# Operands moved to multiples of 64 bytes, and POOL's additions of token blocks spread over slots

## The chip, the cores and the metric

One core of a Trainium2 chip runs the kernel in one launch. The metric is the device time in microseconds from start to end, the median of three runs. TensorE (PE) multiplies, VectorE (DVE), ScalarE (ACT) and GpSimd (POOL) do the element-wise work, and SyncE (SP) issues the transfers. Each engine runs its instructions in the order in which they were written, and waits for others by semaphores.

## What is computed

A clustered attention, then an MLP with a rational activation, then a mixture of eight experts whose gate is balanced by eight Sinkhorn steps. All in float32, with 2 x 768 = 1536 tokens of 512 features.

```python
scores = scale * np.matmul(q, k.transpose(0, 1, 3, 2))   # 2 x 8 heads, 768 x 768, 64 deep
scores = np.where(q_assign == k_assign, scores, -1e9)    # same cluster of 16
x = softmax(scores) @ v                                  # 1536 x 512
h = x @ w_in                                             # 512 -> 2048
x = (P(h) / (Q(h) + 1e-6)) @ w_out                       # cubic by quadratic, 2048 -> 512
P = np.exp(x @ w_gate - max)                             # 1536 x 8
for _ in range(8):
    P /= P.sum(1, keepdims=True) + 1e-9
    P /= P.sum(0, keepdims=True) + 1e-9
    P *= N / E
for e in range(8):
    out += P[:, e:e + 1] * (np.maximum(x @ w1[e], 0.0) @ w2[e])   # 512 -> 1024 -> 512
```

## The kernel before

**Three terms.** Every product of two float32 matrices is made of three matmuls with operands split in a high and a low part: high by high, high by low, low by high (`mm3`, L775). A matmul has a stationary operand, 128 x 128, loaded as weights, and a moving one of up to 512 columns. A profile row names them `out<-moving,stationary`.

**Stages.** (1) Attention, to 287 us: scores `s`, transposes `pt`, the product `v`, and for each pair of heads the cluster matching (`sim` from HQK or LQK, moving, and CH or CL, stationary). (2) The first MLP, 287 to 594 us: eight units of 256 hidden features; each makes `h` from XH, XL (moving) and wh, wl (stationary), the activation in hh and hl, and `y` from hh, hl (moving) and wh, wl (stationary). (3) The first three units of the experts, written out in slots (to 696 us): here `y` has wh, wl moving and hh, hl stationary. (4) `by_seven` (L1056), 29 units: `h` by seven products `m` instead of eight, each of 384 tokens; the sums of token blocks are T2, T3, T4 and those in XH, XL, the sums of weight blocks sh, sl (POOL and ACT make them in `pieces_s`). The results go to gh, gl, which take the buffers of hh, hl, and then 12 tiles of `y` per unit with wh, wl moving and gh, gl stationary, six matmuls a tile.

**Slots.** Stages 2 and 3 are a table: `at(t, key, fn)` (L1162) puts work in slot t, and the loop at L1204 writes out the slots one after the other. A slot of stage 3 holds, in this order: the gathering of the last slot's `y` into acc on DVE (`out2`), the extra work under key "w", twelve matmuls of `h` (`stage1`) with ACT's Relu to hh and DVE's rest to hl, one step of the gate under "g", twelve matmuls of `y` (`stage2`), and the weight work ("W", "l"). t0 (L1186) is the first slot of stage 3, which has 18, t0 to t0 + 17. From t0 + 8 on the gate step is `sink_cols` (on PE the small matmul `sk`, on DVE L767 to L773) and `sink_rows` (DVE L758 to L761): nine DVE instructions, and the next slot's `sk` needs the last, L761.

**The extra work.** `factors` (L918) makes the sums of token blocks, in two halves of 384 tokens. `whole` (L926) adds the high and the low part of a block of XH and XL on POOL (L929) into a tile r; there are four per half, written in two steps a and b. The steps c and d subtract on DVE, d to f split the results (ACT `high`, DVE `low`, L945). L1198 puts a of the first half in slot t0 + 5 and the rest over the slots to t0 + 14. L1200 puts the seven steps of `pieces_s` for the first unit of `by_seven` in slots t0 + 12 to t0 + 15: a and b are four POOL additions into sf, c and d are three ACT casts (rh, sh) and POOL's rl, e is POOL's sl, f and g split that unit's second weights (`split_w`: POOL L634 and L635 on each half).

**Order on POOL.** `split_w` of a unit's second weights is written as soon as a slot comes that has it, but its first instruction waits until PE is done with the unit that had the buffer two units ago; POOL stands still for that long.

**Places in SBUF.** Pools are stacked from the left and from the right; a tile starts where the last one ends, rounded up to 32 bytes. The right stack begins with the attention's pools and, later, those of acc, gate, hh/gh, hl/gl and sg.

Of the kernel before, what the change touches and what calls it, by code (L numbers as in the profile page):

```python
# [9 lines left out]
F32 = mybir.dt.float32  # L10
# [23 lines left out]
def kernel(  # L34
# [16 lines left out]
    P = 128  # L51
# [48 lines left out]
    def right(stack, name, bufs):  # L100
        return stack.enter_context(tc.tile_pool(name=name, bufs=bufs, side="right"))

    def psum(stack, name, bufs):
        return stack.enter_context(tc.tile_pool(name=name, bufs=bufs, space=PSUM))

    stp = right(actx, "stp", 3)
    pp = right(actx, "pp", 6)
    ptp = right(actx, "ptp", 3)
    vsp = right(actx, "vsp", 3)
    sm = right(actx, "sm", 3)  # L110
    xfp = right(actx, "xfp", 2)
    ldp = right(pctx, "ldp", 2)
    one = right(pctx, "one", 1)
# [9 lines left out]
    NB = 4 * NT  # L123
# [47 lines left out]


    csq = one.tile([P, D], F32, name="csq")
    css = one.tile([P, 1], F32, name="css")
    nc.scalar.activation(csq, cen, AF.Square, accum_out=css)
    cnm = one.tile([P, 1], F32, name="cnm")
    gt(cnm, css, half[:, 0:1], op=ALU.pow)
    nc.vector.tensor_scalar(cnm, cnm, 1e-6, None, op0=ALU.add)
    crn = one.tile([P, 1], F32, name="crn")
    nc.vector.reciprocal(crn, cnm)  # L180
    cn2 = one.tile([P, 2, D], F32, name="cn2")
    for j in range(2):
# [67 lines left out]
    def prep(n):  # L250

        b, hp = pairs[n]
# [4 lines left out]
        st = {}  # L257
# [73 lines left out]
            (nc.vector.tensor_tensor if n == 0 else gt)(sv, sv, rev, op=ALU.mult)  # L331

        def classify_d():
            mk = st["mk"] = one.tile([P, NB], F32, tag="mk", name=f"mk_{n}")
            nc.vector.tensor_reduce(mk, st["sv"], axis=AX.X, op=ALU.max)

        def classify_e():
# [31 lines left out]
        def vsplit(j):  # L369
# [19 lines left out]
            (None, classify_m),  # L389
            (None, classify_c),  # L390
            (None, classify_d),
            (classify_e, onehot if n == 0 else lambda: (onehot(), hot.append(onehot_out))),
            *([(onehot_out, None)] if n == 0 else []),
# [21 lines left out]
        return ps  # L415

    def maxima(g, i, ps):
        nm = sm.tile([P, 1], F32, tag="nm", name=f"nm_{g}_{i}")
        nc.vector.tensor_reduce(nm, ps[:, :, :HS], axis=AX.XY, op=ALU.max, negate=True)  # L419
        return nm  # L420

# [93 lines left out]
    def attention():  # L515
# [23 lines left out]
        for kk in range(END + LAGT + 9):  # L539
# [25 lines left out]
            if kk < END:  # L565
                top[kk] = maxima(*divmod(kk, GT), score[kk])
# [112 lines left out]
    for kk in attention():  # L679
# [5 lines left out]
        x = kk - LASTK  # L685
# [212 lines left out]
    PER = NCH * FT  # L898
    N1 = NU1 * PER
    NCL = 3  # L900
    NO = NU1 + NCL
# [12 lines left out]
    def xraw(k, t, j):  # L914
        c = slice(t * HT + j * JT, t * HT + (j + 1) * JT)
        return XH[:, k * K2 : (k + 1) * K2, c], XL[:, k * K2 : (k + 1) * K2, c]

    def factors():  # L918

        st = {}  # L920
        vec = nc.vector.tensor_tensor

        def half(j):
            js = slice(j * JT, (j + 1) * JT)

            def whole(k, t):  # L926
                h, l = xraw(k, t, j)
                r = st[k, t] = wq.tile([P, K2, JT], F32, tag=f"rh{t}", name=f"r_{k}{t}_{j}")
                gt(r, h.bitcast(F32), l.bitcast(F32), op=ALU.add)  # L929

            def parts(n):
                if n not in xop:
                    xop[n] = (
                        xt.tile([P, K2, HT], F32R, tag=f"t{n}h" if n < 4 else "t3", name=f"T{n}h"),
                        xt.tile([P, K2, HT], F32R, tag=f"t{n}l", name=f"T{n}l"),
                    )
                h, l = xop[n]
                return h[:, :, js], l[:, :, js]

            def high(n, r):  # L940
                nc.scalar.copy(parts(n)[0], r)

            def low(n, r):
                h, l = parts(n)
                vec(l, r, h.bitcast(F32), op=ALU.subtract)  # L945

            def a():
                whole(0, 1)
                whole(0, 0)

            def b():
                whole(1, 1)
                whole(1, 0)

            def c():
                for k in range(K2):
                    r = sums[j, k] = cp.tile([P, JT], F32, tag=f"u{2 * j + k}", name=f"T1_{j}_{k}")
                    vec(r, st[0, 1][:, k], st[0, 0][:, k], op=ALU.subtract)
                vec(st[0, 1], st[1, 1], st[0, 1], op=ALU.subtract)

            def d():
                for k in range(K2):
                    vec(st[1, 1][:, k], st[1, 1][:, k], sums[j, k], op=ALU.subtract)
                vec(st[1, 0], st[1, 1], st[1, 0], op=ALU.subtract)
                high(3, st[0, 1])

            def e():
                high(2, st[1, 1])
                high(4, st[1, 0])
                low(3, st[0, 1])  # L970

            def f():
                low(2, st[1, 1])
                low(4, st[1, 0])

            return [a, b, c, d, e, f]

        return half(0) + half(1)

    def first_factor():  # L980
# [6 lines left out]
    def pieces_s(ui):  # L987

        st = {}

        def a():
            st["w"] = staged.pop((ui, 0))
            st["s"] = cp.tile([P, 4, K2, P], F32, tag="sf", name=f"sf_{ui}")
            w, s_ = st["w"], st["s"]
            gt(s_[:, 0], w[:, 0:K2, P:], w[:, K2:, P:], op=ALU.add)
            gt(s_[:, 1], s_[:, 0], w[:, 0:K2, :P], op=ALU.subtract)

        def b():
            w, s_ = st["w"], st["s"]
            gt(s_[:, 2], w[:, 0:K2, :P], w[:, 0:K2, P:], op=ALU.subtract)  # L1000
            gt(s_[:, 3], w[:, K2:, :P], s_[:, 1], op=ALU.subtract)

        def c():
            w = st["w"]
            rh = wq.tile([P, 3, K2, P], F32R, tag="rh0", name=f"rh_{ui}")
            rl = wq.tile([P, 3, K2, P], F32R, tag="rh1", name=f"rl_{ui}")
            sh = wp.tile([P, 4, K2, P], F32R, tag="wh0", name=f"sh_{ui}")
            sl = wp.tile([P, 4, K2, P], F32R, tag="wl0", name=f"sl_{ui}")
            wop[ui] = (rh, rl, sh, sl)
            nc.scalar.copy(rh[:, 0:2].rearrange("p a k f -> p (a k) f"), w[:, :, :P])  # L1010
            nc.scalar.copy(rh[:, 2], w[:, K2:, P:])

        def d():
            w, s_ = st["w"], st["s"]
            rh, rl, sh, sl = wop[ui]
            f2 = "p a k f -> p (a k) f"
            nc.scalar.copy(sh, s_)
            gt(rl[:, 0:2].rearrange(f2), w[:, :, :P], rh[:, 0:2].rearrange(f2).bitcast(F32), op=ALU.subtract)  # L1018
            gt(rl[:, 2], w[:, K2:, P:], rh[:, 2].bitcast(F32), op=ALU.subtract)

        def e():
            rh, rl, sh, sl = wop[ui]
            gt(sl, st["s"], sh.bitcast(F32), op=ALU.subtract)

        def f():
            st["f"] = split_w(ui, 1)
            st["f"][0]()

        def g():
            st["f"][1]()  # L1030

        return [a, b, c, d, e, f, g]
# [129 lines left out]
    def at(t, key, val):  # L1162
        plan.setdefault(t, {}).setdefault(key, []).append(val)

    for ui in range(NO):
        m = units[ui][0]
        for c in range(NCH):
            for f in range(FT):
                n = ui * PER + c * FT + f
                t = n + m * SHIFT  # L1170
# [6 lines left out]
        t = ui * PER + m * SHIFT  # L1177
# [8 lines left out]
    t0 = N1 + SHIFT  # L1186
# [8 lines left out]
        if it < 7:  # L1195
            at(t0 + 8 + it, "g", lambda it=it: sink_rows(it + 1))
    assert 16 < PER * NCL
    for x, fn in enumerate(factors()):  # L1198
        at(t0 + 5 + x * 10 // 12, "w", fn)
    for x, fn in enumerate(pieces_s(NO)):  # L1200
        at(t0 + PER * (NCL - 1) + x // 2, "w", fn)

    last = t0 + PER * NCL
    for t in range(last):  # L1204
# [10 lines left out]
        if steps:  # L1215
            a, b, c, d = steps
# [65 lines left out]
```

## Time and profile before

| | us |
|---|---|
| three runs: median (lowest to highest) | 1623.37 (1623.31 to 1623.74) |
| the profiled execution | 1621.8 |
| its span, first to last instruction | 1620.0 |
| attention | 0 to 287 |
| first MLP | 287 to 594 |
| three units in slots, with the gate | 594 to 696 |
| `by_seven` | 696 to 1604 |
| last `y` tiles and output | 1604 to 1620 |

Over the span PE is busy for 1557.0 us (96%), DVE for 1211.5 (75%), POOL for 816.3 (50%), ACT for 681.6 (42%). Matmuls overlap: a `y` of 512 columns is listed with 394 ns, but the next one starts far sooner, so PE's pace is read from starts, not from durations. DMA engines are busy for a small share after the attention.

### The profile page before, as it was taken

To read this page: it belongs to the slowest core of one execution; us is meant where nothing else is said; L and a number is where in the kernel's file an instruction comes from. 1 tells how busy PE (TensorE), PEld (TensorE's weight loads), DVE (VectorE), ACT (ScalarE), POOL (GpSimd) and SP (SyncE) were. 2 spreads that over 40 slices of the span, in tenths; PEclk is the share of its full clock that TensorE was granted. 3 is DMA by queue.
4 is the path that set the end of the run, shared out by engine and by line. 5 is a ranking of instruction groups with operands and counts; after the bars stand their busy time and mean duration, and the time that the engine had idled before them with its cause. 6 is when DMAs were issued, how large, how long until landed. Compare 5 with 4: busy or idle time off the path is not lost.

```text
span 1620.0 us, 21142 instructions
## 1 busy us (share of the span) xinstructions
PE 1557.0 (96%) x7780; PEld 1353.5 (84%) x7780; DVE 1211.5 (75%) x1963; ACT 681.6 (42%) x1292; POOL 816.3 (50%) x725
## 2 busy tenths in 40 slices
PE   5999998799999999999999999999999999999999
PEld 5888887577777787788888888888888888888887
DVE  6888888899999957878666666666666666666665
ACT  4999888697777741122221212222121222212121
POOL 5577674698777894333533443353344335334420
PEclk8999999899999999999999999999999999999999
DMA  8556542121112010100110110011011001101102
GB/s 185 129 122 136 133 96 93 62 78 53 52 53 78 14 40 14 39 27 27 40 40 27 37 43 27 27 40 40 27 40 39 27 27 40 40 27 40 39 1 78
DMA packets 70950, 87.96 MB, mean 54 GB/s; under 512 B 29792, under 2 KB 48320, under 8 KB 70848
## 3 DMA queue, kind: packets, MB, share of 16 engines
q1 hardware_dynamic: 70848, 86.63, 19.1%
q8 instruction: 61, 1.00, 0.3%
q14 instruction: 41, 0.34, 0.1%
HBM read 62.97 MB, written 3.19 MB: 41 GB/s over the span
## 4 chain that ended last, share of the span: by engine, by line
PE 77%; DVE 15%; issue 4%; ACT 3%; POOL 0%; DMA 0%; SPq 0%; ACTq 0%; DVEq 0%; POOLq 0%
PE y L776 12%; PE y L778 12%; PE y L777 12%; PE m L778 9%; PE m L776 9%; PE m L777 9%; PE pt L438 2%; DVE acc L879 2%; PE v L460 2%; PE h L776 2%; PE h L777 1%; PE v L461 1%; PE h L778 1%; PE s L413 1%; DVE ptl L448 1%
## 5 line engine op out<-in xcount | busy, mean ns | idle before, releaser
L893 DVE SCALAR_TENSOR_TENSOR acc<-y,gate,acc 128x512 f32<-128x512 f32 x348 | 260.8, 750 | 198.9 <-PE y L778 198.0
L1018 POOL TENSOR_TENSOR rl<-sg,rh 128x512 fp32r<-128x512 f32 x29 | 46.1, 1590 | 540.2 <-ACT rh L1010 523.6
L776 PE MATMUL y<-wh,gh 128*128 128x512 f32 x696 | 275.5, 396 | 0.0
L777 PE MATMUL y<-wl,gh 128*128 128x512 f32 x696 | 274.5, 394 | 0.0
L778 PE MATMUL y<-wh,gl 128*128 128x512 f32 x696 | 274.5, 394 | 0.0
L1079 ACT ACTIVATE gh<-u 128x384 fp32r<-128x384 f32 x58 | 30.5, 525 | 430.2 <-DVE u L1104 430.2
L778 PEld LDWEIGHTS y<-wh,gl 128*128 128x128 f32 x696 | 130.6, 188 | 32.3
L777 PEld LDWEIGHTS y<-wl,gh 128*128 128x128 f32 x696 | 130.4, 187 | 27.0
L776 PEld LDWEIGHTS y<-wh,gh 128*128 128x128 f32 x696 | 130.5, 187 | 26.2
L776 PE MATMUL h<-XH,wh 128*128 128x512 f32 x264 | 106.4, 403 | 22.7 <-DVE hl L847 21.6
L1095 ACT COPY c<-m 128x384 f32<-128x384 f32 x58 | 27.8, 480 | 225.6 <-PE m L778 225.6
L448 DVE TENSOR_TENSOR ptl<-pt,pth 128x384 fp32r<-128x384 f32 x192 | 97.3, 548 | 29.6 <-ACT pth L447 29.5
L1079 ACT ACTIVATE gh<-v 128x384 fp32r<-128x384 f32 x174 | 91.2, 524 | 60.1 <-DVE v L1118 27.6
L1080 DVE SCALAR_TENSOR_TENSOR gl<-v,gh 128x384 fp32r<-128x384 f32 x174 | 115.7, 665 | 0.0
L778 PE MATMUL h<-XH,wl 128*128 128x512 f32 x264 | 103.8, 393 | 1.1 <-POOL wl L666 1.1
L777 PE MATMUL h<-XL,wh 128*128 128x512 f32 x264 | 103.9, 393 | 0.0
L635 POOL TENSOR_TENSOR wl<-sg,wh 128x512 fp32r<-128x512 f32 x70 | 99.0, 1414 | 5.9
L419 DVE TENSOR_REDUCE nm<-s 128x1 f32<-128x768 f32 x96 | 91.0, 948 | 6.7 <-PE s L414 5.9
L438 PE MATMUL pt<-ident,pr 128*128 128x128 f32 x576 | 85.4, 280 | 8.5 <-DVE ptl L448 8.2
L447 ACT CAST pth<-pt 128x384 fp32r<-128x384 f32 x192 | 82.7, 482 | 24.3 <-PE pt L438 23.2
L427 ACT ACTIVATE pr<-s,nm 128x768 f32<-128x768 f32 x96 | 87.7, 913 | 2.2 <-DVE nm L419 1.6
L821 POOL TENSOR_TENSOR uu<-uu,h 128x512 f32<-128x512 f32 x48 | 67.7, 1411 | 37.6 <-ACT uu L819 37.6
(226 smaller groups left out, 4280.9 us busy)
## 6 DMA issues: line engine op xcount, KB each, us to landing
sg<-in_moe_w_dram SPq DMA_DIRECT2D x64, 512.0 KB, 3.7
stg<-in_moe_w_in_dram SPq DMA_DIRECT2D x8, 1024.0 KB, 5.4
stg<-in_moe_w_out_dram SPq DMA_DIRECT2D x8, 1024.0 KB, 4.9
st<-HQK SPq DMA_DIRECT2D x16, 384.0 KB, 4.2
st<-LQK SPq DMA_DIRECT2D x32, 192.0 KB, 4.1
st<-HQK SPq DMA_DIRECT2D x32, 192.0 KB, 4.7
qk<-in_q_dram SPq DMA_DIRECT2D x16, 192.0 KB, 3.0
qk<-in_k_dram SPq DMA_DIRECT2D x16, 192.0 KB, 3.6
```

Source lines behind the costliest of these rows:

```text
L419: nc.vector.tensor_reduce(nm, ps[:, :, :HS], axis=AX.XY, op=ALU.max, negate=True)
L427: nc.scalar.activation(pr, ps[:, :, :HS], AF.Exp, bias=nm, accum_out=rss[n][:, x : x + 1])
L438: nc.tensor.transpose(ps[:, i * P : (i + 1) * P], pv_[:, j * P : (j + 1) * P], ident)
L447: nc.scalar.copy(th[:, jj, :], ps[:, :HS])
L448: nc.vector.tensor_tensor(tl[:, jj, :], ps[:, :HS], th[:, jj, :].bitcast(F32), op=ALU.subtract)
L635: gt(wl[:, c], raw[:, c], wh[:, c].bitcast(F32), op=ALU.subtract)
L776: nc.tensor.matmul(ps, ah, bh, start=first, stop=False)
L777: nc.tensor.matmul(ps, ah, bl, start=False, stop=False)
L778: nc.tensor.matmul(ps, al, bh, start=False, stop=last)
L893: nc.vector.scalar_tensor_tensor(a, ps, p, a, op0=ALU.mult, op1=ALU.add)
L1079: nc.scalar.activation(gh[:, f], c, AF.Relu)
L1080: soon.append(lambda: nc.vector.scalar_tensor_tensor(gl[:, f], c, 0.0, gh[:, f].bitcast(F32), op0=ALU.max, op1=ALU.subtract))
```

## The change

It has three parts.

1. A tile of 8 float32 (32 bytes) is put at the start of the right stack, and some small tiles that were followed by matmul operands get a size that is a multiple of 64 bytes (css, cnm, crn, mk), with a view of the old size; nm gets four buffers instead of three, so that what lies behind it keeps its place. In bytes modulo 128 (from the built programs):

| tiles | before | after |
|---|---|---|
| XH, XL, wh, wl, sh, sl, rh, rl, T2 to T4 | 64 | 64 |
| hh, hl, gh, gl | 32 | 0 |
| st, vs, pth, ptl, pr | 96 | 64 |
| HQK, LQK | 32 | 64 |
| CH, CL | 96 | 0 |
| ident, ones | 0 | 0 |

2. The four additions of a half in `factors` become four steps of their own, and the steps get slots by a list: the first half's additions in t0 + 3, 3, 4, 4 and c to f in t0 + 5 to 8; the second half's additions in t0 + 8, 9, 10, 11 and c to f in t0 + 12 to 15.

3. The seven steps of `pieces_s` go to t0 + 13, 14, 16, 16, 17, 17, 17.

```diff
+    right(ctx, "pad", 1).tile([P, 8], F32, name="pad")
     stp = right(actx, "stp", 3)
...
-    css = one.tile([P, 1], F32, name="css")
+    css = one.tile([P, 16], F32, name="css")[:, :1]
...
-            mk = st["mk"] = one.tile([P, NB], F32, tag="mk", name=f"mk_{n}")
+            mk = st["mk"] = one.tile([P, 32], F32, tag="mk", name=f"mk_{n}")[:, :NB]
...
-        nm = sm.tile([P, 1], F32, tag="nm", name=f"nm_{g}_{i}")
+        nm = sm.tile([P, 1], F32, tag="nm", name=f"nm_{g}_{i}", bufs=4)
...
-            def a():
-                whole(0, 1)
-                whole(0, 0)
-
-            def b():
-                whole(1, 1)
-                whole(1, 0)
-
...
-            return [a, b, c, d, e, f]
+            return [lambda k=k, t=t: whole(k, t) for k in range(2) for t in (1, 0)] + [c, d, e, f]
...
-    for x, fn in enumerate(factors()):
-        at(t0 + 5 + x * 10 // 12, "w", fn)
-    for x, fn in enumerate(pieces_s(NO)):
-        at(t0 + PER * (NCL - 1) + x // 2, "w", fn)
+    for x, fn in zip((3, 3, 4, 4, 5, 6, 7, 8, 8, 9, 10, 11, 12, 13, 14, 15), factors()):
+        at(t0 + x, "w", fn)
+    for x, fn in zip((13, 14, 16, 16, 17, 17, 17), pieces_s(NO)):
+        at(t0 + x, "w", fn)
```

PE's and SP's instructions stand in the same order before and after. On the others the order moves in stage 3 only. The changed file has one line more ahead of these places (L930 is the old L929) and later seven fewer.

On POOL, around the second half's additions (r_01_1 to r_10_1), before; wh_10_0 and wh_10_1 are the first and second weights of the third unit, and each half of a split is one L634 and one L635:

```order
L634 TENSOR_SCALAR wh_10_0_6885<-sg_10_0_6706 128x512
L635 TENSOR_TENSOR wl_10_0_6886<-sg_10_0_6706,wh_10_0_6885 128x512
L634 TENSOR_SCALAR wh_10_1_7039<-sg_10_1_6841 128x512
L635 TENSOR_TENSOR wl_10_1_7040<-sg_10_1_6841,wh_10_1_7039 128x512
L929 TENSOR_TENSOR r_01_1_7045<-XH_80,XL_81 128x768
L929 TENSOR_TENSOR r_00_1_7047<-XH_80,XL_81 128x768
L929 TENSOR_TENSOR r_11_1_7049<-XH_80,XL_81 128x768
L929 TENSOR_TENSOR r_10_1_7051<-XH_80,XL_81 128x768
L634 TENSOR_SCALAR wh_10_1_7039<-sg_10_1_6841 128x512
L635 TENSOR_TENSOR wl_10_1_7040<-sg_10_1_6841,wh_10_1_7039 128x512
```

and after:

```order
L635 TENSOR_SCALAR wh_10_0_6895<-sg_10_0_6710 128x512
L636 TENSOR_TENSOR wl_10_0_6896<-sg_10_0_6710,wh_10_0_6895 128x512
L930 TENSOR_TENSOR r_01_1_6953<-XH_80,XL_81 128x768
L930 TENSOR_TENSOR r_00_1_7003<-XH_80,XL_81 128x768
L635 TENSOR_SCALAR wh_10_1_7047<-sg_10_1_6850 128x512
L636 TENSOR_TENSOR wl_10_1_7048<-sg_10_1_6850,wh_10_1_7047 128x512
L930 TENSOR_TENSOR r_11_1_7053<-XH_80,XL_81 128x768
L635 TENSOR_SCALAR wh_10_1_7047<-sg_10_1_6850 128x512
L636 TENSOR_TENSOR wl_10_1_7048<-sg_10_1_6850,wh_10_1_7047 128x512
L930 TENSOR_TENSOR r_10_1_7103<-XH_80,XL_81 128x768
```

Two additions moved ahead of the split of wh_10_1, one between its halves, one behind it.

On DVE, in slot t0 + 9, from the last `y` of slot t0 + 8 on, before:

```order
L887 COPY acc_4053<-y_8_2_3_6984 128x512
L945 TENSOR_TENSOR T2l_6941<-r_11_0_6792,T2h_6940 128x2x384
L945 TENSOR_TENSOR T4l_6944<-r_10_0_6794,T4h_6943 128x2x384
L806 SCALAR_TENSOR_TENSOR hl_9_1_6948<-h_9_1_1_6997,hh_9_1_6947 128x512
L767 TENSOR_REDUCE cs_1_7014<-sk_1_7012 128x8
L770 TENSOR_SCALAR cs_1_7014<-cs_1_7014 128x8
L771 RECIPROCAL cs_1_7014<-cs_1_7014 128x8
L772 TENSOR_SCALAR cs_1_7014<-cs_1_7014 128x8
L773 TENSOR_TENSOR gate_4054<-gate_4054,cs_1_7014 128x96
```

and after:

```order
L888 COPY acc_4057<-y_8_2_3_6992 128x512
L807 SCALAR_TENSOR_TENSOR hl_9_1_6956<-h_9_1_1_7005,hh_9_1_6955 128x512
L768 TENSOR_REDUCE cs_1_7022<-sk_1_7020 128x8
L771 TENSOR_SCALAR cs_1_7022<-cs_1_7022 128x8
L772 RECIPROCAL cs_1_7022<-cs_1_7022 128x8
L773 TENSOR_SCALAR cs_1_7022<-cs_1_7022 128x8
L774 TENSOR_TENSOR gate_4058<-gate_4058,cs_1_7022 128x96
```

T2l and T4l of the first half (step f) moved to slot t0 + 8, and the gate chain from L767 on follows hl.

On ACT, from the last cast of the second half's sums (T4h) on, before:

```order
L941 CAST T4h_6943<-r_10_1_7051 128x2x384
L1010 CAST rh_11_7210<-sg_11_0_6991 128x512
L1011 CAST rh_11_7210<-sg_11_0_6991 128x256
L1017 CAST sh_11_7212<-sf_11_7156 128x1024
L805 ACTIVATE hh_10_0_7161<-h_10_0_1_7219 128x512
L805 ACTIVATE hh_10_1_7270<-h_10_1_0_7272 128x512
L805 ACTIVATE hh_10_1_7270<-h_10_1_1_7320 128x512
```

and after:

```order
L942 CAST T4h_6904<-r_10_1_7103 128x2x384
L806 ACTIVATE hh_10_1_7258<-h_10_1_0_7260 128x512
L806 ACTIVATE hh_10_1_7258<-h_10_1_1_7308 128x512
L1003 CAST rh_11_7347<-sg_11_0_6999 128x512
L1004 CAST rh_11_7347<-sg_11_0_6999 128x256
L1010 CAST sh_11_7349<-sf_11_7206 128x1024
L806 ACTIVATE hh_10_2_7356<-h_10_2_0_7358 128x512
```

The casts of rh and sh moved behind the Relu of three more slots, T4h behind one.

## Rows read from the trace of the kernel before

**Rows 1.** Busy times by stage: span, then each engine (instructions), PEclk, DMA, GB/s

```profile
640.00:696.00 56.00, 49.04 (x211) 39.28 (x210) 46.35 (x97) 10.38 (x18) 21.95 (x21) 0.97 0.09 29
696.00:1604.00 908.00, 908.00 (x4509) 813.80 (x4508) 608.65 (x997) 192.84 (x373) 340.81 (x304) 1.00 0.10 33
```

**Rows 2.** The same view, three units of the first MLP

```profile
399.80:510.66 110.86, 103.24 (x433) 80.17 (x432) 110.65 (x145) 82.85 (x127) 86.32 (x55) 1.00 0.18 59
```

**Rows 3.** Timeline of PE: start us, us, instruction; first and last of 48 h

```profile
286.78 0.39 PE L776 MATMUL h<-XH,wh 128*128 128x512 f32 x1
...
297.43 0.39 PE L778 MATMUL h<-XH,wl 128*128 128x512 f32 x1
```

**Rows 4.** Timeline of PE: first of 18 y, and the m behind them

```profile
1006.22 0.40 PE L776 MATMUL y<-wh,gh 128*128 128x512 f32 x1
...
1010.41 0.33 PE L776 MATMUL m<-XH,rh 128*128 128x384 f32 x1
```

**Rows 5.** Timeline of PE: first and tenth y of a group, first MLP

```profile
404.22 0.40 PE L776 MATMUL y<-hh,wh 128*128 128x512 f32 x1
...
406.32 0.40 PE L776 MATMUL y<-hh,wh 128*128 128x512 f32 x1
```

**Rows 6.** Timeline of PE: four starts of sim apart, five of v

```profile
93.06 0.33 PE L297 MATMUL sim<-HQK,CL 128*128 128x384 f32 x1
...
93.75 0.34 PE L297 MATMUL sim<-LQK,CH 128*128 128x384 f32 x1
...
285.74 0.33 PE L460 MATMUL v<-pth,vs 128*128 128x384 f32 x1
...
286.60 0.34 PE L461 MATMUL v<-ptl,vs 128*128 128x384 f32 x1
```

**Rows 7.** Groups of instructions on DVE, first MLP: busy us, mean ns, idle before

```profile
L844 DVE TENSOR_TENSOR res<-uu,q 128x512 f32<-128x512 f32 x48 | 32.4, 675 | 0.3
L840 DVE TENSOR_TENSOR hh<-uu,h 128x512 fp32r<-128x512 f32 x48 | 32.4, 674 | 4.8 <-POOL uu L822 4.8
```

**Rows 8.** Waits (us, times, longest), timeline of PE, busy times of a stretch

```profile
PE sk L765 <- DVE gate L761: 7.0, 3, 4.4
...
643.78 0.39 PE L778 MATMUL h<-XH,wl 128*128 128x512 f32 x1
...
649.40:652.70 3.30, 3.30 (x9) 2.54 (x8) 3.02 (x12) 0.00 (x0) 1.80 (x3) 0.50 0.46 155
```

**Rows 9.** Timeline of DVE: T4l, the late gate chain, an undisturbed one

```profile
638.53 2.59 DVE L945 TENSOR_TENSOR T4l<-r,T4h 128x768 fp32r<-128x768 f32 x1
...
641.64 0.24 DVE L767 TENSOR_REDUCE cs<-sk 128x8 f32<-128x96 f32 x1
...
644.68 1.81 DVE L773 TENSOR_TENSOR gate<-gate,cs 128x96 f32<-128x96 f32 x1
...
647.29 1.13 DVE L761 TENSOR_TENSOR gate<-gate,rs 128x96 f32<-128x96 f32 x1
...
657.39 0.25 DVE L767 TENSOR_REDUCE cs<-sk 128x8 f32<-128x96 f32 x1
...
659.38 0.26 DVE L761 TENSOR_TENSOR gate<-gate,rs 128x96 f32<-128x96 f32 x1
```

**Rows 10.** Timeline of POOL: additions of both halves, a half split

```profile
603.53 7.24 POOL L929 TENSOR_TENSOR r<-XH,XL 128x768 f32<-128x768 f32 x4
...
635.80 0.62 POOL L634 TENSOR_SCALAR wh<-sg 128x512 fp32r<-128x512 f32 x1 [17.54 <-PE y L778]
636.50 1.29 POOL L635 TENSOR_TENSOR wl<-sg,wh 128x512 fp32r<-128x512 f32 x1
637.75 8.62 POOL L929 TENSOR_TENSOR r<-XH,XL 128x768 f32<-128x768 f32 x4
```

**Rows 11.** Groups of instructions on ACT and POOL in by_seven

```profile
L1017 ACT CAST sh<-sf 128x1024 fp32r<-128x1024 f32 x28 | 29.0, 1035 | 0.0
...
L1023 POOL TENSOR_TENSOR sl<-sf,sh 128x1024 fp32r<-128x1024 f32 x28 | 76.3, 2726 | 0.0
```

More of the change, by code (lines that the diff above doesn't have):

```diff
@@ L173 @@
     csq = one.tile([P, D], F32, name="csq")
-    css = one.tile([P, 1], F32, name="css")
+    css = one.tile([P, 16], F32, name="css")[:, :1]
     nc.scalar.activation(csq, cen, AF.Square, accum_out=css)
-    cnm = one.tile([P, 1], F32, name="cnm")
+    cnm = one.tile([P, 16], F32, name="cnm")[:, :1]
     gt(cnm, css, half[:, 0:1], op=ALU.pow)
     nc.vector.tensor_scalar(cnm, cnm, 1e-6, None, op0=ALU.add)
-    crn = one.tile([P, 1], F32, name="crn")
+    crn = one.tile([P, 16], F32, name="crn")[:, :1]
     nc.vector.reciprocal(crn, cnm)
```

## The prediction

> **What bounds the kernel now.** I read the profile stage by stage: first the busy times of each engine in the stages, then the starts of single matmuls, because the durations of pipelined matmuls overlap and only the distance from one start to the next is time that is paid. From 696 to 1604 us, the loop `by_seven`, PE is busy for 908.00 of 908.00 us and no other engine comes near [rows 1]: a nanosecond on each matmul there is a nanosecond on the end. Between 640 and 696 us PE is busy for 49.04 of 56.00 us [rows 1], so it waits for something. In the first MLP it is different again: in three of its units DVE is busy for 110.65 of 110.86 us [rows 2], and PE follows it. So there are two questions: what one matmul costs in the last 908 us, and what PE waits for ahead of them.
>
> **One matmul.** Where `h` is made, 512 columns at a time, 47 starts take 297.43 - 286.78 = 10.65 us, 226.6 ns each [rows 3]. Where `y` is made in `by_seven`, with 512 columns and three terms too, 18 starts take 1010.41 - 1006.22 = 4.19 us, 232.8 ns each [rows 4]. What differs is the place of the operands. For `h` the moving operand (XH, XL) and the stationary one (wh, wl) both lie 64 past a multiple of 128 bytes. For `y` the moving one (wh, wl) does too, but the stationary one (gh, gl) lies 32 past, so the two stand 32 bytes apart. In the first MLP's `y` the moving operand (hh, hl) is the displaced one, and there nine starts take 406.32 - 404.22 = 2.10 us, 233.3 ns each [rows 5]: the same surcharge from the other side. The displacement by itself does not cost it: in the attention both operands of `v` lie 32 past a multiple of 64, and five starts of 384 columns take 0.86 us, 172 ns each [rows 6]; 226.6 ns less 128 columns at 2.4 GHz (53.3 ns) is 173. So I read it as a surcharge on the distance between the two read streams, 232.8 - 226.6 = some 6.3 ns on 512 columns.
>
> **Part 1, the pad and the tile sizes.** After the change gh and gl lie at multiples of 128 and wh, wl still 64 past one: the distance goes from 32 to 64. The trace has no 512-column matmul at that distance; the nearest row is `sim` with 384, HQK at 32 and CH at 96 past a multiple of 128, where four starts take 93.75 - 93.06 = 0.69 us, 172 ns each [rows 6], no surcharge. So I take it as gone, 226.6 ns; the ends that I keep are no change at all and the same 6.3 ns on the other side.
> - `by_seven`: 29 units x 12 tiles x 6 = 2088 matmuls of `y` x 6.3 ns = 13.2 us, all on the path [rows 1].
> - The three plain units ahead of it: 36 tiles x 6 = 216 x 6.3 ns, 1.3 us on PE's path between its waits.
> - The first MLP: 576 x 6.7 ns would be 3.9 us, but DVE is the bound there [rows 2]. I take 0: DVE's own work covers it, and 3.9 us is the end of the range if it does not.
> - The attention: scores and `v` have distance 0 before and after; 0.
> - Other engines use the moved tiles too. On DVE, L840 writes hh (at 32) in 674 ns and L844 writes res (at 0) in 675 ns [rows 7]; a moved tile is worth nothing there, and I take the same for ACT and POOL. The wider css, cnm, crn and mk, the pad and the fourth buffer of nm change no instruction and no order: 0.
>
> The Trainium skill has a rule against this part. "TensorE: Matmul & The Clock Gate", Part 2, the first of its steps, says that PE reads the moving operand and the weights through two independent ports, so that loading the next weights takes no bandwidth from the running matmul. By it no distance between the two could matter, and part 1 would be worth 0. The rows of `h` and `y` do differ [rows 3, 4], so I keep it as a rival only.
>
> **Part 2, one addition per slot.** Ahead of `by_seven` PE waits for the gate at `sk`: 7.0 us in three waits, the longest 4.4, until L761 [rows 8], the last of a chain of nine small DVE instructions. Undisturbed the chain takes 659.38 + 0.26 - 657.39 = 2.25 us; in the late one it takes 647.29 + 1.13 - 641.64 = 6.78, L773 alone 1.81, and ahead of it T4l takes 2.59 [rows 9]. All that time POOL is in four additions of L929 in a row, 8.62 us, and L773 ends at 646.49, 0.1 us behind them (646.37) [rows 9, 10]. I read it so: a DVE instruction whose operands lie in SBUF waits until the POOL instruction that is running ends. After the wait the granted clock is 0.50, the 1.2 GHz level, for the 3.3 us of [rows 8], which costs half of that, 1.6 us; 0.97 over the stage [rows 1] is one such stretch. Together 8.6 us.
>
> After the change two of these four additions stand on POOL ahead of the split of wh_10_1, for which POOL waits until 635.80 [rows 10], and fall into idle time; the other two alternate with the split's halves; and T2l and T4l leave this slot of DVE. POOL's run from 635.80 on is two halves (0.62 + 1.29 each) and two additions (7.24 / 4 = 1.81 undisturbed [rows 10]), 7.4 us, where it was 12.4. I laid the chain over that run: it starts when hl is done, no longer behind T2l and T4l; L772 then waits for a half, L773 for the last addition, until 643.2, and the rest for what POOL does next. By this estimate it ends near 644.8, 0.8 us after PE is ready (643.78 + 0.23 [rows 8]); I take a wait of 1.0 us, and the clock as staying up. The two later waits go: the casts of rh and sh move behind three more hh on ACT, and with them rl, sl and the second weights' split move behind the last gate chain. Gain 8.6 - 1.0 = 7.6 us; the ends are 8.6 (no wait) and 2.6 (the long wait stays, with its clock).
>
> Who waits for what was moved: `by_seven` needs sl for its second product. Three casts (sh's is the longest, 1.04 us), rl and sl (sl's is the longest, 2.73 us [rows 11]) are under 8.6 us behind slot 15's hh, and PE still has two and a half slots to run, each 12 x 226.6 + 12 x 226.6 ns = 5.4 us: 13 us. That cover of 5 us gone, the loop would start late by what is missing, once. DVE's c, d, e, f stand a slot earlier (first half) or later (second), as much work in a slot as before, in slots where PE did not wait for it: 0.
>
> **Sum.** 13.2 + 1.3 + 7.6 = 22.1 us. The profiled execution took 1621.8 us (span 1620.0) and would take 1599.7; the median of the three timed runs is 1623.37, and there it is 1601.3 us. A measurement of this kernel can tell 0.2%, 3.2 us, from no change.
>
> **Rivals.**
> - Phase stays: the surcharge has another cause, `y` keeps 232.8 ns, and part 2 alone works. For it: no 512-column row at distance 64, and 384 columns may hide a surcharge that 512 show. Against it: `sim`, and the same surcharge for both kinds of `y`. 1623.4 - 7.6 = 1615.8. The Trainium skill would have it so by a second rule: "SBUF — State Buffer", Specifications (TRN2), gives lines of 16 bytes, and to these an offset of 32 is as good as one of 64.
> - Stall moves: part 1 works, but POOL is still busy for 7.4 us in a row, and if the chain meets it at every link, as before, `sk` waits its 4.4 us, the clock falls, and the later waits come back beside wh_10_1 and sf. 1623.4 - 14.5 = 1608.9.
> - Slower: the surcharge grows with the distance, and 64 costs twice what 32 does. Then 2088 + 216 `y` cost another 6.3 ns each, 14.5 us, against the 7.6 of part 2: 1623.4 + 6.9 = 1630.3. It decides from 7.6 us / 2304 = 3.3 ns more on each `y`, at 236 ns. `sim` speaks against it.
> - Neither does what it says: `y` stays and the stall moves; 1623.4, within 0.2%.
>
> **How the numbers follow.** Forecast 0.64, phase stays 0.14, stall moves 0.12, slower 0.06, neither 0.04. The forecast's own range is 1597 (no wait left, and the first MLP gives most of its 3.9 us) to 1607 (the long wait stays). The range goes on to 1616.5 and takes in the second and third case: 1597 to 1616.5. Faster by over 0.2%: 0.90; within 0.2%: 0.04; slower: 0.06.
>
> **What would show it.** Right: `y` starts 226 to 227 ns apart in `by_seven`; that loop 13 us shorter; one `sk` wait of about 1 us and no stretch at clock 0.50 between 640 and 660 us; the first MLP as long as before. Wrong: `y` at 233 ns or more; the chain to L761 still over 4 us beside POOL's additions; PE idle at the start of `by_seven`.

## The result, and the profile after

The changed kernel takes 1604.16 us (median of four runs, 1603.78 to 1604.57) beside 1623.55 for the kernel before on the same chip: a ratio of 0.988, 95% interval 0.9863 to 0.9897. The prediction was 1601.3, in a range of 1597 to 1616.5. The profiled execution has a span of 1602.3 us where it was 1620.0, 17.7 less; the medians lie 19.4 apart, because the profiled execution of before was 1.6 us under the median of its timed runs, and this difference is not traced to a place.

Busy times of the changed kernel by stretch (span, then PE, PEld, DVE, ACT, POOL with instructions, PEclk, DMA, GB/s): the end of the three units, `by_seven`, and three units of the first MLP, which answer to [rows 1, 2].

```profile
640.00:686.00 46.00, 45.02 (x203) 36.91 (x203) 38.99 (x90) 9.82 (x17) 16.38 (x17) 1.00 0.11 35
686.00:1586.00 900.00, 900.00 (x4511) 814.56 (x4511) 611.08 (x998) 193.36 (x375) 341.22 (x304) 1.00 0.10 33
398.90:510.00 111.10, 103.14 (x434) 80.09 (x433) 110.89 (x145) 83.06 (x128) 86.70 (x55) 1.00 0.17 57
```

PE now idles for 1 us in the first stretch, its clock is 1.00 there, PE is the bound in `by_seven` as before, and DVE in the first MLP as before.

Timeline of PE of the changed kernel (start us, us, instruction): the first and the tenth `y` of a group in the first MLP, the first `y` of a group in `by_seven` and the `m` behind its 18, against [rows 5] and [rows 4].

```profile
403.58 0.39 PE L777 MATMUL y<-hh,wh 128*128 128x512 f32 x1
...
405.68 0.39 PE L777 MATMUL y<-hh,wh 128*128 128x512 f32 x1
...
1001.59 0.39 PE L777 MATMUL y<-wh,gh 128*128 128x512 f32 x1
...
1005.72 0.33 PE L777 MATMUL m<-XH,sh 128*128 128x384 f32 x1
```

In the first MLP nine starts still take 2.10 us, 233.3 ns each: nothing has changed there. In `by_seven` 18 starts take 4.13 us, 229 ns each, where they took 4.19. Over all 2088 the three lines differ: y<-wh,gh starts 229 ns before its follower, y<-wl,gh 232, y<-wh,gl 226, in an exact cycle of three. So the surcharge is neither gone nor kept.

The three stages end here (same view, the last `y` of the first MLP, the first `m` and the last `y` of all), first in the changed kernel and then in the kernel before:

```profile
593.36 0.39 PE L779 MATMUL y<-hh,wl 128*128 128x512 f32 x1
...
686.98 0.33 PE L777 MATMUL m<-XH,rh 128*128 128x384 f32 x1
...
1598.25 0.39 PE L779 MATMUL y<-wh,gl 128*128 128x512 f32 x1
```

```profile
593.93 0.40 PE L778 MATMUL y<-hh,wl 128*128 128x512 f32 x1
...
696.01 0.33 PE L776 MATMUL m<-XH,rh 128*128 128x384 f32 x1
...
1615.94 0.39 PE L778 MATMUL y<-wh,gl 128*128 128x512 f32 x1
```

From the first to the second is the stage of the three units, 93.6 us where it was 102.1; from the second to the third `by_seven` with its last tiles, 911.3 us where it was 919.9. These two lengths are used for all experiments below, since they leave out the attention: the first `h` behind it starts between 286.0 and 288.3 us in the profiled executions of this document, before and after, so its length is not put down to the change.

The stall, in waits of PE (us, times, longest), PE's timeline around it, then DVE's and POOL's:

```profile
PE sk L766 <- DVE gate L762: 1.0, 1, 1.0
```

```profile
643.01 0.39 PE L779 MATMUL h<-XH,wl 128*128 128x512 f32 x1
644.37 0.43 PE L766 MATMUL sk<-gate,ones 128*128 128x96 f32 x2 [0.97 <-DVE gate L762]
```

```profile
639.73 1.10 DVE L773 TENSOR_SCALAR cs<-cs 128x8 f32<-128x8 f32 x1
640.86 1.85 DVE L774 TENSOR_TENSOR gate<-gate,cs 128x96 f32<-128x96 f32 x1
...
643.64 0.59 DVE L762 TENSOR_TENSOR gate<-gate,rs 128x96 f32<-128x96 f32 x1
```

```profile
639.51 1.29 POOL L636 TENSOR_TENSOR wl<-sg,wh 128x512 fp32r<-128x512 f32 x1
640.76 1.84 POOL L930 TENSOR_TENSOR r<-XH,XL 128x768 f32<-128x768 f32 x1
```

One wait of 1.0 us is left of the three in [rows 8]. The chain has the shape that the prediction laid out: L773 ends with the half split (640.83 and 640.80 us), L774 (1.85 us) with the last addition (1.84 us; 642.71 and 642.60), and L762 is done at 644.23.

### The profile page after: what moved, and what is told of

It reads as the page before. It is cut to its first block, busy times and chain, and to the rows that moved or that the text cites. A ratio compares the mean times of both kernels' runs of the same rounds, so it can differ in the third digit from the quotient of the medians.

```text
span 1602.3 us, 21124 instructions
## 1 busy us (share of the span) xinstructions
PE 1545.0 (96%) x7780; PEld 1351.9 (84%) x7780; DVE 1208.5 (75%) x1963; ACT 682.4 (43%) x1292; POOL 815.9 (51%) x725
## 4 chain that ended last, share of the span: by engine, by line
PE 76%; DVE 14%; issue 4%; ACT 3%; POOL 2%; DMA 0%; SPq 0%; ACTq 0%; DVEq 0%; POOLq 0%
PE y L778 12%; PE y L777 12%; PE y L779 11%; PE m L779 9%; PE m L777 9%; PE m L778 9%; PE pt L439 2%; DVE acc L880 2%; PE v L461 2%; PE v L462 1%; PE s L414 1%; PE h L777 1%; DVE ptl L449 1%; DVE q L827 1%; PE h L778 1%
## 5 line engine op out<-in xcount | busy, mean ns | idle before, releaser
L779 PE MATMUL y<-wh,gl 128*128 128x512 f32 x696 | 270.2, 388 | 0.0
```

The source lines that it names most:

```text
L779: nc.tensor.matmul(ps, al, bh, start=False, stop=last)
```

## Experiments

**The two parts apart.** `places_only` has the pad and the tile sizes with the old lists of slots; `slots_only` has the new lists with the old places:

```diff
-    for x, fn in zip((3, 3, 4, 4, 5, 6, 7, 8, 8, 9, 10, 11, 12, 13, 14, 15), factors()):
-        at(t0 + x, "w", fn)
-    for x, fn in zip((13, 14, 16, 16, 17, 17, 17), pieces_s(NO)):
-        at(t0 + x, "w", fn)
+    for x, fn in enumerate(factors()):
+        at(t0 + 5 + x * 10 // 12, "w", fn)
+    for x, fn in enumerate(pieces_s(NO)):
+        at(t0 + PER * (NCL - 1) + x // 2, "w", fn)
```

> Only the places of the operands are changed (pad and tile sizes); the slots of GpSimd's additions and of the first unit's pieces are those of the kernel before. Theory (the two parts are independent): y as in the changed kernel, 229, 232 and 226 ns for its three lines in by_seven, which makes that loop about 8.5 us and the y of the three units about 0.7 us shorter; the long wait at sk (4 to 5 us), the stretch at clock 0.50 and the later waits stay. About 1623.5 - 9.2 = 1614.3 us. Rival (most of the gain of by_seven comes from the new slots, because its weights are ready when it starts): y stays near 233 ns and the time is 1622 or more.

> Only the slots are changed; all operands lie where they lay in the kernel before. Theory: y stays at 233 ns in by_seven and in the three units; one wait at sk of about 1.1 us is left, no stretch at clock 0.50, and the three units end about 7.8 us earlier: about 1623.5 - 7.8 = 1615.7 us. Rival (the shorter y moved PE against DVE and did part of it): the wait at sk is longer than 2 us and the time is above 1618.

Waits of PE and the ends of the stages, `places_only`, then `slots_only`:

```profile
PE sk L766 <- DVE gate L762: 7.0, 3, 4.4
```

```profile
696.09 0.33 PE L777 MATMUL m<-XH,rh 128*128 128x384 f32 x1
...
1607.35 0.39 PE L779 MATMUL y<-wh,gl 128*128 128x512 f32 x1
```

```profile
PE sk L765 <- DVE gate L761: 1.0, 1, 1.0
```

```profile
688.53 0.33 PE L776 MATMUL m<-XH,rh 128*128 128x384 f32 x1
...
1608.46 0.39 PE L778 MATMUL y<-wh,gl 128*128 128x512 f32 x1
```

| kernel | median us | ratio to before (95%) | three units | `by_seven` to last `y` | waits at `sk` |
|---|---|---|---|---|---|
| before | 1623.18 | 1 | 102.1 | 919.9 | 7.0 |
| places_only | 1614.44 | 0.9945 (0.993 to 0.9959) | 101.7 | 911.3 | 7.0 |
| slots_only | 1613.55 | 0.994 (0.9925 to 0.9954) | 94.1 | 919.9 | 1.0 |
| changed | 1604.16 | 0.988 (0.9863 to 0.9897; its before: 1623.55) | 93.6 | 911.3 | 1.0 |

The parts are independent: the places are worth 8.6 us in `by_seven` and 0.4 in the units, the slots 8.0 us in the units and nothing in `by_seven`. Both rivals fall. The expectation for `slots_only`, 1615.7, was 2 us too high; by the stages it gained 8.0 instead of 7.8, and the rest lies between medians and profiled executions and is not traced.

**What distance is free.** In `shift64` and `shift192` a second pad moves hh, hl, gh and gl alone:

```diff
+    right(ctx, "pad2", 1).tile([P, 16], F32, name="pad2")    # 48 in shift192
     hb = right(ctx, "hb", 3)
```

> The changed kernel with 64 bytes more ahead of hh, hl, gh, gl: the distance from the stationary gh, gl to the moving wh, wl is then 0 modulo 128 and 128 modulo 256 (changed kernel: 64 modulo 128; before: 96 modulo 128). Theory A (what costs is the distance modulo 128, and only 0 is free): y starts 226 to 227 ns apart on all three lines in by_seven, 2088 x 2.2 = 4.6 us less there and some 0.8 us less in the three units, and the y of the first MLP at 226.6 ns without a gain in time: about 1598.8 us. Theory B (a longer period): y stays at 228 ns or more, 1603 or more. Theory C (only the stationary operand's own place counts, and 64 is enough): as the changed kernel, 229, 232 and 226 ns, 1604.2 us.

> The changed kernel with 192 bytes more ahead of hh, hl, gh, gl: the distance from gh, gl to wh, wl is then 0 modulo 512, as between XH and wh, where h is made. Theories A and B (distance): y starts 226 to 227 ns apart in by_seven and in the first MLP, about 1598.8 us; A and B differ in shift64 alone. Theory C (only the stationary operand's own place counts, and 64 is enough): as the changed kernel, 1604.2 us. If y still takes more than 228 ns on two of its lines, no distance explains it and another cause must be sought, such as the order in which the three terms follow each other.

They took 1611.92 us (ratio 0.9928, 0.9914 to 0.9943) and 1603.01 (0.9873, 0.9856 to 0.9889). So 0 modulo 128 is not enough (theory A falls), and 0 modulo 512 gave only a fifth of the gain expected (1.15 us under the changed kernel instead of 5.4). None of that fifth is in `by_seven`, which takes 911.2 us in `shift192` beside 911.3 (918.3 in `shift64`). Timeline of PE, `shift64`: first `y` of a group and the `m` behind its 18.

```profile
1005.15 0.39 PE L778 MATMUL y<-wh,gh 128*128 128x512 f32 x1
...
1009.33 0.34 PE L778 MATMUL m<-XH,sh 128*128 128x384 f32 x1
```

`shift192`: two `y` of the first MLP, nine starts apart, then the first and the tenth `y` of a group in `by_seven` and the `m` behind it:

```profile
404.13 0.39 PE L778 MATMUL y<-hh,wh 128*128 128x512 f32 x1
...
406.17 0.39 PE L778 MATMUL y<-hh,wh 128*128 128x512 f32 x1
...
1008.91 0.39 PE L778 MATMUL y<-wh,gh 128*128 128x512 f32 x1
...
1010.99 0.39 PE L778 MATMUL y<-wh,gh 128*128 128x512 f32 x1
...
1013.03 0.33 PE L778 MATMUL m<-XH,rh 128*128 128x384 f32 x1
```

At distance 0 the first nine `y` of a group take 2.08 us, 231 ns each, and the other nine 2.04 us, 226.7 each. In the first MLP, too, they take 2.04 us where they took 2.10. So distance 0 is free once the stream has settled, and in `by_seven`, where groups of 18 `y` follow `m` of 384 columns, half of each group goes by before it has. That makes the mean 228.9 ns over 18, the same as in the changed kernel, which never settles and pays in a cycle of three. `shift64` takes 4.18 us for 18, 232 ns.

Three more kernels give the three buffers of gh (and of gl) three distances in one kernel, by a larger tile for each buffer and a pool of its own for hl and gl, with pads between:

```diff
-    hb = right(ctx, "hb", 3)
+    right(ctx, "pad2", 1).tile([P, 64], F32, name="pad2")
+    hbl = right(ctx, "hbl", 3)
+    right(ctx, "pad3", 1).tile([P, 80], F32, name="pad3")
+    hb = right(ctx, "hb", 3)
+
+    def part(pool, tag, name, n):
+        return pool.tile([P, FT * 512 + 16], F32R, tag=tag, name=name)[:, : FT * n].rearrange(
+            "p (f n) -> p f n", f=FT
+        )
...
-                            hb.tile([P, FT, JT], F32R, tag="hh", name=f"gh_{ui}_{j}_{t}"),
-                            hb.tile([P, FT, JT], F32R, tag="hl", name=f"gl_{ui}_{j}_{t}"),
+                            part(hb, "hh", f"gh_{ui}_{j}_{t}", JT),
+                            part(hbl, "hl", f"gl_{ui}_{j}_{t}", JT),
```

(the second of the three; the others have 8 for 16 and pads of 16 and 104, and of 48 and 104). Each was run once, so they are read by their starts and not by their times.

> The changed kernel with the three buffers of hh (gh) and of hl (gl) each at another distance from the moving wh, wl: stationary less moving address is 32, 64 and 96 modulo 512 for units that follow each other. So far by_seven's y takes, as a mean of a group: 233 ns at 224 (before), 229 at 192 (changed kernel), 232 at 128 (shift64), and at 0 (shift192) it starts with nine slower ones and then stays at 226.7. Theory P256 (the cost repeats every 256 bytes and only 0 settles at 226.7): 229 ns or more at all three. Theory SMALL (near distances are as good as 0, since the weights are read just behind or ahead of the moving stream): 32 and 64 settle at 226.7. Theory SIZE (what counts is the largest power of two that divides the distance): 32 and 96 like 224, 233 ns; 64 like 192, 229 ns.

> As the run before, with distances of 256, 320 and 384 modulo 512. Theory P256 (the cost repeats every 256 bytes): 256 settles at 226.7 ns like 0, 384 is like 128 (232 ns, never settling), 320 is 228 ns or more. Theory P512: 256 does not settle. Theory SIZE (the largest power of two that divides the distance): 320 like 192 (229 ns), 384 like 128 (232), 256 better than both.

> As the two runs before, with distances of 416, 448 and 480 modulo 512. Theory P256 (the cost repeats every 256 bytes): 448 shows the three lines of the changed kernel, 229, 232 and 226 ns; 480 shows the 233 ns of the kernel before; 416 is 228 or more. Theory SIZE: 448 the same, 416 and 480 both 233. Theory P512: none of them has to look like an earlier one.

Timeline of PE, `map_256_320_384`: first `y` of a group and the `m` behind its 18, for 320, 256 and 384 in this order.

```profile
1003.66 0.39 PE L786 MATMUL y<-wh,gh 128*128 128x512 f32 x1
...
1007.86 0.34 PE L786 MATMUL m<-XH,sh 128*128 128x384 f32 x1
...
1012.04 0.39 PE L786 MATMUL y<-wh,gh 128*128 128x512 f32 x1
...
1016.16 0.33 PE L786 MATMUL m<-XH,rh 128*128 128x384 f32 x1
...
1019.31 0.39 PE L786 MATMUL y<-wh,gh 128*128 128x512 f32 x1
...
1023.48 0.34 PE L786 MATMUL m<-XH,sh 128*128 128x384 f32 x1
```

18 starts take 4.20, 4.12 and 4.17 us. The same rows of `map_32_64_96` at 64 and of `map_416_448_480` at 448, 4.20 and 4.12 us:

```profile
1006.39 0.39 PE L786 MATMUL y<-wh,gh 128*128 128x512 f32 x1
...
1010.59 0.34 PE L786 MATMUL m<-XH,sh 128*128 128x384 f32 x1
```

```profile
1005.12 0.39 PE L786 MATMUL y<-wh,gh 128*128 128x512 f32 x1
...
1009.24 0.33 PE L786 MATMUL m<-XH,sh 128*128 128x384 f32 x1
```

Every group of one distance agrees with the others within 0.1 ns, so a table can be made, of the stationary operand's address less the moving one's (from the built programs), modulo 256, and the mean from one start to the next over a group of 18:

| distance | 0 | 32 | 64 | 96 | 128 | 160 | 192 | 224 |
|---|---|---|---|---|---|---|---|---|
| ns | 228.9 | 233.2 | 233.3 | 234.0 | 232.0 | 233.3 | 228.9 | 233.0 |
| seen at (modulo 512) | 0, 256 | 32 | 64, 320 | 96 | 128, 384 | 416 | 192, 448 | 224 (before), 480 |

P256 holds in every pair that was run: 256 settles as 0 does, 448 has the changed kernel's cycle of three, 384 repeats `shift64`, 480 the kernel before; 32, 96 and 160 were seen at one distance each. SMALL falls (32 and 64 cost all of it), and so does SIZE: 64 and 192 have the same power of two and cost 233.3 and 228.9. These two are 64 to either side of 0, so the distance has a sign. In `by_seven` the moving operand always lies in the same place, so these groups alone could as well show the stationary operand's own place. The first MLP parts the two: there the tiles have the opposite roles, wh and wl stay where they are as the stationary operand, and the pace still follows the distance. hh at 32 modulo 128 made it 32, [rows 5], the change made it 64, which costs the same 233.3, and `shift192` made it 0, 226.7. At 192, in two of the three kernels above, the starts there come to the cycle of 229, 232 and 226 ns as well, after some four slower ones. Why these values and not others cost is not shown by any run here.

**What the slots did.** Three kernels, each run once, undo one piece of part 2 in the changed kernel: the four additions together again, the old slots for `pieces_s`, or T2l and T4l back in the slot of the late chain.

```diff
-    for x, fn in zip((3, 3, 4, 4, 5, 6, 7, 8, 8, 9, 10, 11, 12, 13, 14, 15), factors()):
+    for x, fn in zip((3, 3, 4, 4, 5, 6, 7, 8, 10, 10, 10, 10, 12, 13, 14, 15), factors()):
```

> The changed kernel with the four GpSimd additions of the second half in one slot again (t0 + 10, between the halves of a split), and everything else as changed: T2l and T4l of the first half stay out of the slot, the first unit's pieces stay late. Theory (a DVE instruction on SBUF operands waits for the running GpSimd instruction): the gate chain of that slot runs into four additions in a row, L774 and L762 of it take over 1 us each, sk waits 3 to 4.5 us once and the clock falls to 0.50 behind it; the units end 3.5 to 5 us later than in the changed kernel (span about 1606 to 1607). Rival (what made the chain late were T2l and T4l ahead of it): the wait at sk stays at 1 us or so and the span near 1602.3. With either, the two later waits do not come back.

```diff
-    for x, fn in zip((13, 14, 16, 16, 17, 17, 17), pieces_s(NO)):
-        at(t0 + x, "w", fn)
+    for x, fn in enumerate(pieces_s(NO)):
+        at(t0 + PER * (NCL - 1) + x // 2, "w", fn)
```

> The changed kernel with the steps of the first unit's pieces in their old slots (t0 + 12 to t0 + 15); the additions stay spread. Theory: the two later waits at sk (0.5 and 2.4 us before the change) come back and the first stays at 1.0 us, so the units end about 2.9 us later, span about 1605.2. Rival (the later waits came from the long one, which put PE ahead of or behind the other engines): they stay away, span about 1602.3.

```diff
-    for x, fn in zip((3, 3, 4, 4, 5, 6, 7, 8, 8, 9, 10, 11, 12, 13, 14, 15), factors()):
+    for x, fn in zip((3, 3, 4, 4, 5, 6, 7, 9, 8, 9, 10, 11, 12, 13, 14, 15), factors()):
```

> The changed kernel with the last step of the first half (T2l and T4l on DVE) back in slot t0 + 9, ahead of hl and the gate chain; the additions stay spread. Theory: these two take 2 to 4 us beside GpSimd's work and push the chain behind them, so sk waits 2.5 to 4 us instead of 1.0 and the clock falls to 0.50 behind it: span 1605 to 1608. Rival (only GpSimd's additions in a row counted): the wait stays near 1 us, span about 1602.3.

| kernel | three units, us | more than changed | waits at `sk` |
|---|---|---|---|
| changed | 93.6 | | 1.0 |
| additions_together | 98.6 | 5.0 | 3.0 |
| pieces_old | 95.1 | 1.5 | 2.3 in two |
| t4_back | 93.8 | 0.2 | 1.1 |

`additions_together`: POOL, then DVE beside it, then the busy times from the end of the wait on.

```profile
637.90 7.23 POOL L930 TENSOR_TENSOR r<-XH,XL 128x768 f32<-128x768 f32 x4
```

```profile
640.14 1.44 DVE L771 TENSOR_SCALAR cs<-cs 128x8 f32<-128x8 f32 x1
641.62 0.20 DVE L772 RECIPROCAL cs<-cs 128x8 f32<-128x8 f32 x1
641.85 1.53 DVE L773 TENSOR_SCALAR cs<-cs 128x8 f32<-128x8 f32 x1
643.42 1.82 DVE L774 TENSOR_TENSOR gate<-gate,cs 128x96 f32<-128x96 f32 x1
```

```profile
646.80:653.50 6.70, 6.17 (x16) 4.95 (x17) 5.11 (x15) 0.00 (x0) 3.08 (x5) 0.50 0.24 78
```

Three instructions on 8 to 96 columns end one POOL addition after the other: 641.58, 643.38 and 645.24, and the four additions (1.81 us each) end at 645.13. The RECIPROCAL between them keeps its 0.20 us in the midst of an addition, so it is not every DVE instruction that waits, as the theory was written: here it is TENSOR_SCALAR and TENSOR_TENSOR. The wait is 2.0 us longer, and the granted clock is 0.50, the 1.2 GHz level, for 6.2 us of PE's work behind it, which costs half, 3.1 us: together 5.1, beside the 5.0 (4.94) measured. This is the piece that held most of the stall, as the theory has it. `pieces_old` brought back one later wait, not two, 1.5 us instead of 2.9 (its span is 1606.1, since its first MLP ended 2.3 us later, which has no part in this). There, too, one instruction on 96 columns lasts as long as the POOL instruction beside it:

```profile
672.20 2.40 POOL L1016 TENSOR_TENSOR sl<-sf,sh 128x1024 fp32r<-128x1024 f32 x1
```

```profile
672.30 2.41 DVE L774 TENSOR_TENSOR gate<-gate,cs 128x96 f32<-128x96 f32 x1
```

`t4_back` is a miss. DVE, then POOL:

```profile
637.93 0.96 DVE L946 TENSOR_TENSOR T2l<-r,T2h 128x768 fp32r<-128x768 f32 x1
638.81 0.95 DVE L946 TENSOR_TENSOR T4l<-r,T4h 128x768 fp32r<-128x768 f32 x1
```

```profile
639.03 2.44 POOL L930 TENSOR_TENSOR r<-XH,XL 128x768 f32<-128x768 f32 x1 [0.96 <-DVE T2l L946]
```

T2l and T4l took 0.96 and 0.95 us where T4l alone took 2.59 in [rows 9]; the addition had to wait for T2l and took 2.44 us instead of 1.81, so here POOL was the one that stood still. Counted from the end of the first MLP, the chain began 0.3 us later but took 5.1 us instead of 5.3, and the wait stayed at 1.1 us. The three pieces sum to 6.7 us of the 8.1 between `places_only` and the changed kernel. The other 1.4 come when pieces are undone together, or from the slots that none of the three undoes (the first half's additions and its c to e, the second half's c to f); no run parts these.

**A version of both.** `best` is `shift192` with the second half's last three additions earlier, in t0 + 8, 9 and 9, where the expectation names two of them and puts r_11 in t0 + 8:

```diff
-    for x, fn in zip((3, 3, 4, 4, 5, 6, 7, 8, 8, 9, 10, 11, 12, 13, 14, 15), factors()):
+    for x, fn in zip((3, 3, 4, 4, 5, 6, 7, 8, 8, 8, 9, 9, 12, 13, 14, 15), factors()):
```

> shift192 (distance 0) with the additions r_11 and r_10 of the second half in slots t0 + 8 and t0 + 9, so that all four stand on GpSimd ahead of the split that has to wait, in time in which GpSimd was idle. Theory (each DVE step of the gate chain waits for the GpSimd instruction that runs): no GpSimd addition is left beside the chain that ends late, the last wait at sk (1.0 us) goes, and no other takes its place: about 1 us under shift192, 1602 us. Rival (the additions only meet the chain of the slot before): a wait of about 1 us stays, 1603 us.

> The changed kernel once more, timed beside the run before on the same chip: 1604.2 us by its first timing, so some 2 us above it by the theory and some 1 us by the rival.

1602.79 us (1601.82 to 1602.92) and 1604.14 (1603.45 to 1604.85), ratios to before 0.9873 (0.9856 to 0.9889) and 0.9883 (0.9868 to 0.9898): ahead by 1.35 us with runs that do not overlap, though less than the 0.2% that can be told with confidence. Against `shift192` (1603.01) the moved additions bring nothing that can be told (0.2 us; 0.4 us in the three units of the profiled executions): waits of PE in `best`, and POOL and DVE ahead of it.

```profile
PE sk L767 <- DVE gate L763: 0.7, 1, 0.7
```

```profile
630.88 4.22 POOL L931 TENSOR_TENSOR r<-XH,XL 128x768 f32<-128x768 f32 x2 [2.79 <-DVE T2l L947]
```

```profile
633.61 1.52 DVE L774 TENSOR_SCALAR cs<-cs 128x8 f32<-128x8 f32 x1
...
636.12 0.98 DVE L761 TENSOR_SCALAR rs<-rs 128x12 f32<-128x12 f32 x1
```

The two additions now run beside the chain of the slot before, and that one is late by 0.7 us. A wait of 1.0 us went and one of 0.7 took its place one slot earlier: neither the theory nor the rival as they were written.

## Why the prediction came out as it did

- **`by_seven`, 13.2 us: 8.6.** The step that failed is "I take it as gone, 226.6 ns". The surcharge does hang on the distance between the two operands, as read from [rows 3 to 5], and `places_only` shows its worth without the slots. But the distance counts modulo 256 and with its sign: the change went from 224 to 192, where a `y` takes 228.9 ns on average, 4.1 less than the 233.0 of all groups before, and not 6.3 less. The row that was taken for the distance of 64, `sim` [rows 6], has two starts at 64 and two at 192 modulo 256 in the built program, 170 to 174 ns each; at 64, 512 columns cost all of it (233.3). So these 384 columns did not show the surcharge that 512 have, as the rival "phase stays" allowed, and for the same reason `v`, with 384 columns at distance 0, could not show that a displacement alone is free. The result lies inside the ends that were kept, between the forecast and no change at all.
- **The three units' `y`, 1.3 us: 0.4 to 0.5** (102.1 to 101.7, 94.1 to 93.6), for the same reason.
- **The first MLP, 0: right, but not for the reason given**, 307.3 us from its first `h` to its last `y` where it was 307.2. Its `y` did not get shorter at all, which the prediction had not seen, so the change could not test whether DVE's work covers it. `shift192` did: there they take 226.7 ns, and the stage is 306.2 us long. By that, DVE covers most of the 3.9 us, and some 1 us comes through.
- **The stall, 7.6 us: 8.0** in `slots_only`. Wait, clock and later waits went as laid out; by starts the wait that is left is 1.36 us from the last `h` to `sk` less one start, 0.23: 1.1 us. The reading behind it was too wide, as `additions_together` shows: beside POOL's additions TENSOR_SCALAR and TENSOR_TENSOR stretch (0.17 to 1.53 us, 0.26 to 1.82), TENSOR_REDUCE and RECIPROCAL do not (0.25, 0.20).
- **What was costed at nothing** stayed so: the loop `by_seven` did not start late, with PE busy for 900.00 of 900.00 us from 686 us on.
- **The sum, 22.1 us**, is 17.0 by these terms (8.6 + 0.4 + 8.0), 17.7 in the profiled spans and 19.4 between the medians; the forecast of 1601.3 was 2.9 us low. That it was not further off is in part luck: 1.7 us of the fall of the medians is not in the profiled spans and was in no term. The rivals: "phase stays" (1615.8) and "stall moves" (1608.9) each had one part failing whole, and neither part did. "Slower" and "neither" did not come about either, but `shift64` shows how near "phase stays" lay: 64 bytes more, and `y` is back at 232 ns, 1 ns under the kernel before.

The page of the Trainium skill "TensorE: Matmul & The Clock Gate" (Part 2, first step) says that loading the next weights takes no read bandwidth of SBUF from the running matmul, and "SBUF — State Buffer" (Specifications, TRN2) in the Trainium skill has lines of 16 bytes, to which 32 and 64 are alike. If these two were all that counts, the place of the operands could not matter. The trace does not agree, and it decides: with the order of PE's instructions kept, `y` goes from 226.7 ns (settled, distance 0) to 233.3 (distance 64), by the place of the operands alone. Whether it is the two reads that meet is not shown.

## What to carry to other kernels

Where PE is the bound and matmuls are 512 columns of float32 wide, measure the distance between the stationary and the moving operand, modulo 256 bytes and with its sign, and try a pad: two kernels that differ in one pad of 64 bytes were 7.8 us apart (the changed one and `shift64`), 7.1 of it in `by_seven`. Take the price of a matmul only from a row of the same width, and in groups as short as those of the kernel, since a group may be over before its pace has settled. Where a chain of small DVE instructions feeds PE, spread GpSimd's long instructions so that no two in a row lie beside the chain, and look one slot ahead for the chain that they meet instead.

## What was not expected of the hardware

- Three steady paces are whole numbers of cycles at 2.4 GHz: 226.67 ns (`h`, and `y` settled at distance 0) is 544, which is 512 columns and 32; 173.33 (`m`, settled) is 416, which is 384 and 32; 233.33 (`y` at distance 64) is 560, another 16. The other values of the table are means over starts of unequal length.
- At a distance of 0 a group does not start at its pace: nine `y` take 2.08 us instead of 2.04, in each of the 113 groups that `m` follows. That is some 4.6 us of the 911, and neither its cause nor a way around it was tried.
- The low clock at `sk` lasted longer with the shorter wait: 6.7 us with 3.0 us of waiting in `additions_together`, 3.3 us after 4.4 in [rows 8].
